# Pairing the 64-row ends of a 1728-wide feed-forward, with a longer backward lag

## The chip, the core and the metric

The kernel runs on one core of a Trainium2 chip. Its engines are TensorE (matmul, with a weight load ahead of each matmul), VectorE, ScalarE, GpSimd (POOL) and SyncE, which here only issues DMAs. TensorE writes to PSUM, an accumulator memory, from which VectorE and ScalarE read; everything else lies in SBUF, or in the chip's main memory. The metric is the device time of one execution in microseconds, as a median of several runs.

## The reference

A gated mix of two blocks, run forward and backward in one kernel. x and grad_out are 2048 x 640, all in bf16:

```python
g = sigmoid((x * gate_w).sum(-1, keepdims=True))
a = linear_attention(x, wqkv, wo)      # 32 heads of 20; phi(t) = t+1 or exp(t)
b = relu(x @ w1) @ w2                  # w1 640 x 1728, w2 1728 x 640
out = g * a + (1 - g) * b
```

The outputs are `out` and the gradients of the sum against grad_out: for x, wqkv, wo, w1, w2 and gate_w (`out_0` to `out_6`, in that order).

## The kernel before

The 2048 tokens are 16 tiles of 128 (NT), 640 is 5 blocks of 128 (KD), and F = 1728 is 13 blocks of 128 and one of 64 (KF = 14, FT = 64). The hidden activations of a tile, `hs(i)`, are kept padded to 14 x 128 = 1792 columns; the pad is set to zero by a memset for each group of four tiles (L501). w2's 14th block is padded by a memset (L385), and so is w1's transposed tail (L452, L636).

`mm_cols` (L315) is one product of a stationary 128x128 block with 640 columns: two matmuls, of 512 and 128 columns, into the two banks of one accumulator. Accumulators come from one pool of four, `pp()` (L288). Large SBUF buffers are placed in one arena by a planner from sizes and lifetimes that are written by hand (L116 to L183), in rings of 2 to 4 slots where they rotate.

Stages, in order:
- K chunks and the product Y (L412 to L454), with w1's tail transposed by TensorE in between (L448 to L453).
- Forward, L546 to L558: for each tile `q_main`, `h_half(i, 0)`, `q_post`, `h_half(i, 1)`, then `out_chunk(i - 2)` (LAG = 2). `h_half` ends with a transposing DMA of `hs(i)` into `hTs[i]` (L514), and `out_chunk` multiplies the 14 blocks of it by w2, and five of `pqTs[i]` by M, into one accumulator. `q_store` writes three pairs of tiles through SyncE.
- dW2, L608 to L627: for each of 14 blocks m, 16 tiles are accumulated (L611); between blocks run `r_main` and `r_post`, the start of the attention backward. `r_main` copies a 128x32 result on VectorE (L582).
- X, L637 to L648: five blocks, each sent to `load_T(XT_s...)` at once. Then three more transposing loads, KV2, woT, wvT (L649 to L651).
- Feed-forward backward, L756 to L778: for each tile `fb_a(i)` (two halves of `gp`, masked on VectorE in place of `hs(i)`, then a transposing DMA to `dhTs[i]`), and `fb_b(i - 2)`, 14 blocks of it by w1T into `dp`. Four groups of small products, `small_0` to `small_3`, with the DMAs that they lead to, stand at i = 2, 3, 5 and 8. In the last two rounds `dw1_half` takes `fb_a`'s place.
- dW1 and `dk_chunk` (L779 to L790), dWk, dWq, and dx (L825 to L849), where the last tile's two column parts share one accumulator.

SyncE's transposes and loads go through one queue, ScalarE's stores through another, each in order. The order on a queue is not always that of the text: the tile framework plans each engine's order ahead of time, and moves DMAs forward where it can.

The loop that the diff reorders most, as it stands before:

```python
for i in range(NT + LAG):
    if i < NT:
        fb_a(i)
    else:
        dw1_half(i - NT)
    ...
    if i >= LAG:
        fb_b(i - LAG)
```

Of the kernel before, what the change touches and what calls it, by code (L numbers as in the profile page):

```python
# [77 lines left out]
def kernel(  # L78
# [73 lines left out]
    ar.add("X", KD * D * B2, T_X, T_FB + 22)  # L152
    ar.add("XT", KD * D * B2, T_X + 5, T_FB + 25)
    ar.add("KV2", KD * D * B2, T_FB, T_FB + 22)
    ar.add("woT", KD * D * B2, T_FB, T_FB + 25)
    ar.add("wvT", KD * D * B2, T_FB + 5, T_FB + 45)
    ar.add("YT", KD * D * B2, T_FB + 30, T_FB + 60)
    ar.add("dKV", KD * D * B2, T_FB + 30, T_FB + 60)
    ar.add("dKVT", KD * D * B2, T_FB + 22, T_FB + 45)
    ar.add("Q", KD * D * B2, T_FB + 25, T_DWK - 10)  # L160
    ar.add("N", KD * D * B2, T_DWK, T_END)
    ring("hTb", KF * P, 3, T_FB, T_DW1 + 5)
    ring("wst", D, 4, T_FB, T_FB + 60)
    ar.add("dwoT", KD * D * B2, T_FB + 10, T_FB + 50)
    ar.add("dwo", KD * D * B2, T_FB + 22, T_FB + 60)
# [219 lines left out]
    nc.gpsimd.memset(w2_s[:, KF - 1, :], 0.0)  # L385
    nc.sync.dma_start(w2_s[:FT, KF - 1, :], B_w2[(KF - 1) * P:F, :])

# [47 lines left out]
    for m in range(KD):  # L435
# [12 lines left out]
        if m == 2:  # L448
            tp = psp.tile([P, KD, P], BF16, tag="PP", bufs=4, name="w1ttp")
            for k in range(KD):  # L450
                nc.tensor.transpose(tp[:FT, k, :], w1_s[:, k, (KF - 1) * P:F], ident[:])
            nc.vector.memset(w1T_tail[:], 0.0)  # L452
            nc.vector.tensor_copy(w1T_tail[:FT, :], tp[:FT].rearrange("p k d -> p (k d)"))  # L453
# [45 lines left out]
    def h_half(i, half):  # L499
        if i % G == 0 and half == 0:  # L500
            nc.gpsimd.memset(hsg[i // G][:, :, F:FPAD], 0.0)  # L501
# [9 lines left out]
        else:  # L511
            nc.vector.tensor_scalar(dst, hp[:, :, 0:NBW], omg_t[:, i:i + 1], 0.0, ALU.mult, ALU.max)
            hTs[i] = rnext("hTf").rearrange("p (c s) -> p c s", s=P)
            load_T(hTs[i], hs(i))  # L514

    def out_chunk(i):
        pr, ii = i // 2, i % 2
        op = pp("op")
        hT, pqT = hTs.pop(i), pqTs.pop(i)
        for kf in range(KF):  # L520
            mm_cols(op, hT[:, kf, :], lambda a, e: w2_s[:, kf, a:e], kf == 0, False)
        for k in range(KD):
            mm_cols(op, pqT[:, k, :], lambda a, e: M_s[:, k, a:e], False, k == KD - 1)
# [22 lines left out]
    for i in range(1, NT + LAG):  # L546
        if i < NT:
            q_main(i)
            h_half(i, 0)
            q_post(i)  # L550
            h_half(i, 1)
        if i % 2 == 0 and i <= NT:
            q_store(i // 2 - 1)
        if i >= LAG:
            out_chunk(i - LAG)
        if i == NT - 1:
# [12 lines left out]
    def r_main(i):  # L569
# [12 lines left out]
        nc.vector.tensor_copy(doX[:, i, D:DX], w32[:])  # L582
# [25 lines left out]
    for m in range(KF):  # L608
        wp = pp("w2p")
        for i in range(NT):  # L610
            mm_cols(wp, hs(i)[:, csl(m)], lambda a, e: doX[:, i, a:e], i == 0, i == NT - 1)  # L611
        st = rnext("w2st")
        nc.scalar.copy(st, flat(wp)[:, 0:D])
        rows = P if m < KF - 1 else FT
        nc.scalar.dma_start(out_5[m * P:m * P + rows, :], st[:rows, :])
        while 0 < m and done < NT and done < m * NT / (KF - 3):
# [20 lines left out]
    for m in range(KD):  # L637
# [10 lines left out]
        load_T(XT_s[:, :, csl(m)], X_s[:, m, :])  # L648
    load_T(KV2_s, KVT_d)  # L649
    load_T(woT_s, A_wo)  # L650
    load_T(wvT_s, A_wqkv[:, 2 * D:3 * D])  # L651
# [4 lines left out]
    def fb_a(i):  # L656
        for half in range(2):
            gp = pp("gp")
            for nb in range(2):
                blk = 2 * half + nb  # L660
                for k in range(KD):
                    nc.tensor.matmul(gp[:, nb, 0:NBW], lhsT=doTg[i // G][:, k, gsl(i)],  # L662
                                     rhs=w2T_s[:, k, blk * NBW:(blk + 1) * NBW], start=(k == 0), stop=(k == KD - 1))
            rng = slice(2 * half * NBW, (2 * half + 2) * NBW)
            gs = tmp("tb", 8, [P, 2, NBW])
# [219 lines left out]
```

## Time and profile before

| what | value |
|---|---|
| median of 3 runs | 658.83 us (658.72 to 659.83) |
| the profiled execution | 659.8 us, of which the span of the trace is 657.9 |
| granted TensorE clock over the span | 0.995 |
| DMA | 108.19 MB moved; SyncE's queue took 59.5% of the 16 engines' span |

Busy time of each engine by stage (us from the start; TensorE is PE):

| stage | stretch | PE | VectorE | ScalarE | POOL | DMA share |
|---|---|---|---|---|---|---|
| K chunks | 0 to 34 | 31.6 of 34.0 | 24.8 | 15.0 | 26.0 | 0.98 |
| Y | 34 to 61 | 23.0 of 27.0 | 19.9 | 2.3 | 5.4 | 0.57 |
| forward | 69.5 to 227.1 | 157.6 of 157.6 | 70.8 | 36.4 | 61.3 | 0.65 |
| X | 311.2 to 334 | 22.8 of 22.8 | 1.8 | 3.5 | 0.0 | 0.44 |
| dW1, dk | 477 to 545 | 68.0 of 68.0 | 24.3 | 6.7 | 0.0 | 0.59 |
| dWk, dWq | 545 to 588.7 | 43.7 of 43.7 | 3.1 | 7.1 | 0.0 | 1.09 to 1.13 |
| dx | 588.7 to 657.9 | 65.7 of 69.2 | 25.0 | 1.0 | 0.0 | 0.13 |

Between these lie dW2 (227.1 to 311.2; PE 82.8 of 84.1, VectorE 55.2, ScalarE 20.6) and the feed-forward backward (334 to 477; PE 140.1 of 143.0, VectorE 35.6, ScalarE 52.0, DMA share 0.83).

How to read it: matmuls are pipelined, and one lasts longer in the records (379 ns for 512 columns, 219 for 128) than it keeps the next one waiting. So the pace of TensorE is read from the distance of starts. A line such as `170.92 5.33 PE L317 MATMUL op_1823<-arena ... x38` is a group of 38 matmuls that started at 170.92 us, over 5.33 us. In brackets behind such a line stand the idle time before it and what ended it. "arena" names any buffer of the large SBUF block. A wait is put down to whichever of its releasers came last.

### The profile page before, as it was taken

The page shows a single profiled execution, that of the slowest core. Times are in us where ns is not written, and L with a number is a line of the kernel's source. Part 1 is how long each engine was busy: PE and PEld are TensorE (multiplying, and loading weights), DVE is VectorE, ACT ScalarE, POOL GpSimd, SP SyncE. Part 2 cuts the span into 40 slices and gives each one's busy share as a digit, 9 for nine tenths or more (in the row PEclk, how much of TensorE's full clock was granted, in tenths as well). Part 3 has the DMA queues.
Part 4 walks back from the last instruction along what each step waited for, and adds up shares of the span by engine and source line. Part 5 has one row for each costly group of instructions (what it writes and reads, how often), then busy time and mean ns, then how long its engine had stood idle before and what let it go on. Part 6 is the DMA issues. An engine that isn't in the chain of part 4 may idle for free.

```text
span 657.9 us, 10575 instructions
## 1 busy us (share of the span) xinstructions
PE 643.6 (98%) x4475; PEld 362.2 (55%) x4475; DVE 266.3 (40%) x503; ACT 148.1 (23%) x193; POOL 120.3 (18%) x115
## 2 busy tenths in 40 slices
PE   8979999999999999999999999999999999999997
PEld 5546555555555555555555545555555555555554
DVE  5994654445445137785034322222043320104442
ACT  4401321222212122322133435333101111020000
POOL 6931444334343112332001000000000000000000
PEclk9979999999999999999999999999999999999999
DMA  9991863664738999326389999934186439991111
GB/s 258 319 354 60 212 159 101 146 153 122 177 74 227 280 239 253 115 81 155 81 171 192 271 256 277 237 81 96 53 190 121 118 92 225 215 254 41 41 41 41
DMA packets 229049, 108.19 MB, mean 164 GB/s; under 512 B 181770, under 2 KB 228362, under 8 KB 229002
## 3 DMA queue, kind: packets, MB, share of 16 engines
q1 hardware_dynamic: 217114, 92.93, 59.5%
q10 hardware_dynamic: 11888, 14.59, 7.0%
q8 instruction: 35, 0.57, 0.4%
q14 instruction: 12, 0.10, 0.0%
HBM read 31.46 MB, written 30.97 MB: 95 GB/s over the span
## 4 chain that ended last, share of the span: by engine, by line
PE 87%; DMA 5%; DVE 5%; issue 1%; SPq 1%; ACT 1%; ACTq 0%; DVEq 0%
DMA arena<-arena 3%; DVE arena L362 2%; PE yp_531 L317 1%; PE w1p_5247 L750 1%; PE w1p_5122 L750 1%; PE w1p_4985 L750 1%; PE w1p_5190 L750 1%; PE w1p_5054 L750 1%; PE w1p_4916 L750 1%; PE w1p_4847 L750 1%; PE w1p_4761 L750 1%; PE w1p_4661 L750 1%; PE w1p_4596 L750 1%; DMA arena<-pqg_d 1%; PE op_2304 L317 1%
## 5 line engine op out<-in xcount | busy, mean ns | idle before, releaser
L317 PEld LDWEIGHTS <-arena 128*128 128x128 bf16 x2914 | 226.3, 98 | 183.4 <-issue 9.0
L750 PEld LDWEIGHTS <-arena 128*128 128x128 bf16 x320 | 30.9, 98 | 26.6
L662 PEld LDWEIGHTS <-arena 128*128 128x128 bf16 x320 | 30.7, 98 | 26.4
L506 PEld LDWEIGHTS <-arena 128*128 128x128 bf16 x320 | 30.6, 98 | 26.2
L406 POOL TENSOR_TENSOR arena<-arena 128x640 f32<-128x640 f32 x14 | 19.7, 1409 | 5.1 <-DVE arena L362 4.4
L641 PEld LDWEIGHTS <-arena 128*128 128x128 bf16 x80 | 7.8, 98 | 9.4
L815 PEld LDWEIGHTS <-arena 128*128 128x128 bf16 x80 | 7.8, 98 | 9.5
L828 DVE SCALAR_TENSOR_TENSOR f_5652<-gwb,dl_t,arena 128x640 f32<-128x640 bf16 x1 | 0.9, 884 | 28.7 <-DMA arena<-dxB_d 28.7
L693 POOL MEMSET arena<- 128x3200 bf16 x1 | 2.8, 2764 | 40.0 <-PE dwo_3583 L339 40.0
L734 DVE TENSOR_TENSOR tb_4739<-dkp_4728,dzb 128x640 bf16<-128x640 f32 x1 | 0.8, 825 | 22.8 <-PE dkp_4728 L317 22.8
L317 PE MATMUL yp_489<-arena 128*128 128x512 bf16 (+1 forms) x32 | 4.9, 308 | 4.0 <-DVE arena L362 4.0
L339 PEld LDWEIGHTS <-arena 128*128 128x128 bf16 x140 | 7.8, 97 | 1.9 <-issue 0.8
L642 PEld LDWEIGHTS <-arena 128*128 128x128 bf16 x80 | 7.8, 98 | 0.0
L816 PEld LDWEIGHTS <-arena 128*128 128x128 bf16 x80 | 7.8, 98 | 0.0
L317 PE MATMUL yp_531<-arena 128*128 128x512 bf16 (+1 forms) x32 | 6.6, 387 | 0.0
L750 PE MATMUL w1p_4596<-arena 128*128 128x432 bf16 x32 | 6.0, 346 | 0.0
L750 PE MATMUL w1p_4916<-arena 128*128 128x432 bf16 x32 | 6.0, 346 | 0.0
L750 PE MATMUL w1p_4985<-arena 128*128 128x432 bf16 x32 | 6.0, 346 | 0.0
L750 PE MATMUL w1p_5122<-arena 128*128 128x432 bf16 x32 | 6.0, 346 | 0.0
L750 PE MATMUL w1p_5247<-arena 128*128 128x432 bf16 x32 | 6.0, 346 | 0.0
L750 PE MATMUL w1p_4661<-arena 128*128 128x432 bf16 x32 | 6.0, 346 | 0.0
L750 PE MATMUL w1p_4761<-arena 128*128 128x432 bf16 x32 | 6.0, 346 | 0.0
(1026 smaller groups left out, 1208.4 us busy)
## 6 DMA issues: line engine op xcount, KB each, us to landing
out_dram<-arena ACTq DMA_DIRECT2D x28, 160.0 KB, 3.9
pk_d<-arena SPq DMA_DIRECT2D x4, 640.0 KB, 9.6
arena<-in_grad_out_dram SPq DMA_DIRECT2D x8, 320.0 KB, 4.6
pqg_d<-arena SPq DMA_DIRECT2D x8, 320.0 KB, 4.4
e_d<-arena SPq DMA_DIRECT2D x8, 320.0 KB, 4.0
out_dram<-arena ACTq DMA_DIRECT2D x8, 320.0 KB, 3.4
arena<-pqg_d SPq DMA_DIRECT2D x4, 640.0 KB, 5.5
arena<-e_d SPq DMA_DIRECT2D x8, 320.0 KB, 3.5
```

The costliest lines, as they stand in the source:

```text
L317: nc.tensor.matmul(ps_tile[:, b, 0:e - a], lhsT=lhsT, rhs=rhs_fn(a, e), start=start, stop=stop, **kw)
L339: nc.tensor.matmul(ps_tile[:, bank, a - 512 * bank:e - 512 * bank], lhsT=lhsT_fn(j), rhs=rhs_mat[:, j, a:e], start=bank not in seen, stop= ...
L362: nc.vector.scalar_tensor_tensor(dst, ps_flat, 1.0 + 1e-6, cp[:], ALU.add, ALU.max)
L406: nc.gpsimd.tensor_tensor(zacc, zacc, pkN[:, i, :], ALU.add)
L506: nc.tensor.matmul(hp[:, nb, 0:NBW], lhsT=xT(i, k), rhs=w1_s[:, k, blk * NBW:(blk + 1) * NBW], start=(k == 0), stop=(k == KD - 1))
L641: nc.tensor.matmul(xp[:, 0, :], lhsT=lhsT, rhs=doX[:, i, 0:512], start=(i == 0), stop=(i == NT - 1))
L642: nc.tensor.matmul(xp[:, 1, 0:DX - 512], lhsT=lhsT, rhs=doX[:, i, 512:DX], start=(i == 0), stop=(i == NT - 1))
L662: nc.tensor.matmul(gp[:, nb, 0:NBW], lhsT=doTg[i // G][:, k, gsl(i)], rhs=w2T_s[:, k, blk * NBW:(blk + 1) * NBW], start=(k == 0), stop=(k ...
L693: nc.gpsimd.memset(dKVT_s, 0.0)
L750: nc.tensor.matmul(wp[:, nb, 0:NBW], lhsT=xN2[:, i, csl(m)], rhs=hs(i)[:, blk * NBW:(blk + 1) * NBW], start=(i == 0), stop=(i == NT - 1))
L815: nc.tensor.matmul(wp[:, 0, :], lhsT=lhsT, rhs=dqN[:, i, 0:512], start=(i == 0), stop=(i == NT - 1))
L816: nc.tensor.matmul(wp[:, 1, 0:D + 1 - 512], lhsT=lhsT, rhs=dqN[:, i, 512:D + 1], start=(i == 0), stop=(i == NT - 1))
```

## The change

The pad of `hs(i)` and of w2's and w1T's last block is no longer zero but a second copy of the 64 real rows. The 14th block of two neighbouring tiles is then multiplied in one go: `tail_pair` uses partitions 0 to 63 for the even tile and 64 to 127 for the odd one, into two accumulators. In dW2's last block even tiles write accumulator rows 0 to 63 and odd tiles rows 64 to 127, and the halves are added afterwards. In the forward loop, `h_half(i, 1)` of odd tiles moves behind `out_chunk`. In the backward loop the lag becomes four tiles, with a ring of five for dhT, `fb_a` is called by halves, and the transposes and stores around the small products are spread over the iterations. `r_main` starts one block later, its 128x32 copy goes to ScalarE, and the last tile's second part gets its own accumulator. Lifetimes in the arena follow (most of those lines are left out here).

```diff
-    ar.add("X", KD * D * B2, T_X, T_FB + 22)
-    ar.add("XT", KD * D * B2, T_X + 5, T_FB + 25)
+    ar.add("X", KD * D * B2, T_X, T_FB + 24)
+    ar.add("XT", KD * D * B2, T_FB + 5, T_FB + 50)
...
-    ring("hTb", KF * P, 3, T_FB, T_DW1 + 5)
-    ring("wst", D, 4, T_FB, T_FB + 60)
-    ar.add("dwoT", KD * D * B2, T_FB + 10, T_FB + 50)
-    ar.add("dwo", KD * D * B2, T_FB + 22, T_FB + 60)
+    ring("hTb", KF * P, 5, T_FB, T_DW1 + 5)
+    ring("wst", D, 4, T_FB + 88, T_FB + 112)
...
-    nc.gpsimd.memset(w2_s[:, KF - 1, :], 0.0)
     nc.sync.dma_start(w2_s[:FT, KF - 1, :], B_w2[(KF - 1) * P:F, :])
+    nc.sync.dma_start(w2_s[FT:, KF - 1, :], B_w2[(KF - 1) * P:F, :])
...
                 nc.tensor.transpose(tp[:FT, k, :], w1_s[:, k, (KF - 1) * P:F], ident[:])
-            nc.vector.memset(w1T_tail[:], 0.0)
-            nc.vector.tensor_copy(w1T_tail[:FT, :], tp[:FT].rearrange("p k d -> p (k d)"))
+                nc.tensor.transpose(tp[FT:, k, :], w1_s[:, k, (KF - 1) * P:F], ident[:])
+            nc.vector.tensor_copy(w1T_tail[:], tp.rearrange("p k d -> p (k d)"))
...
     def h_half(i, half):
-        if i % G == 0 and half == 0:
-            nc.gpsimd.memset(hsg[i // G][:, :, F:FPAD], 0.0)
...
+            nc.vector.tensor_copy(hs(i)[:, F:FPAD], hs(i)[:, F - FT:F])
             hTs[i] = rnext("hTf").rearrange("p (c s) -> p c s", s=P)
             load_T(hTs[i], hs(i))
...
+    def tail_pair(psA, psB, lA, lB, rhs, last):
+        for b, (a, e) in enumerate(DSPL):
+            nc.tensor.matmul(psA[:, b, 0:e - a], lhsT=lA[0:FT], rhs=rhs[0:FT, a:e], start=False, stop=last)
+            nc.tensor.matmul(psB[:, b, 0:e - a], lhsT=lB[FT:P], rhs=rhs[FT:P, a:e], start=True, stop=False)
+    ops = {}
     def out_chunk(i):
         pr, ii = i // 2, i % 2
-        op = pp("op")
         hT, pqT = hTs.pop(i), pqTs.pop(i)
-        for kf in range(KF):
-            mm_cols(op, hT[:, kf, :], lambda a, e: w2_s[:, kf, a:e], kf == 0, False)
+        if ii == 0:
+            ops[i] = pp("op")
+        op = ops.pop(i)
+        for kf in range(KF - 1):
+            mm_cols(op, hT[:, kf, :], lambda a, e: w2_s[:, kf, a:e], ii == 0 and kf == 0, False)
         for k in range(KD):
-            mm_cols(op, pqT[:, k, :], lambda a, e: M_s[:, k, a:e], False, k == KD - 1)
+            mm_cols(op, pqT[:, k, :], lambda a, e: M_s[:, k, a:e], False, ii == 1 and k == KD - 1)
+        if ii == 0:
+            ops[i + 1] = pp("op")
+            tail_pair(op, ops[i + 1], hT[:, KF - 1, :], hTs[i + 1][:, KF - 1, :], w2_s[:, KF - 1, :], True)
         if ii == 0:
             o_st[pr] = rnext("ost").rearrange("p (i d) -> p i d", i=2)
         nc.scalar.copy(o_st[pr][:, ii, :], flat(op)[:, 0:D])
@@ -548,11 +560,14 @@
             q_main(i)
             h_half(i, 0)
...
-            h_half(i, 1)
+            if i % 2 == 0 or i == NT - 1:
+                h_half(i, 1)
         if i % 2 == 0 and i <= NT:
             q_store(i // 2 - 1)
         if i >= LAG:
             out_chunk(i - LAG)
+        if i < NT - 1 and i % 2 == 1:
+            h_half(i, 1)
...
-        nc.vector.tensor_copy(doX[:, i, D:DX], w32[:])
+        nc.scalar.copy(doX[:, i, D:DX], w32[:])
...
+        if m < KF - 1:
+            for i in range(NT):
+                mm_cols(wp, hs(i)[:, csl(m)], lambda a, e: doX[:, i, a:e], i == 0, i == NT - 1)
+            nc.scalar.copy(st, flat(wp)[:, 0:D])
+            nc.scalar.dma_start(out_5[m * P:(m + 1) * P, :], st)
+        else:
+            for i in range(0, NT, 2):
+                for b, (a, e) in enumerate(DSPL):
+                    for t in range(2):
+                        nc.tensor.matmul(wp[t * FT:(t + 1) * FT, b, 0:e - a], lhsT=hs(i + t)[:, m * P:F],
+                                         rhs=doX[:, i + t, a:e], start=(i == 0), stop=(i == NT - 2),
+                                         skip_group_check=True)
+            w2e = tmp("f32", 3, dt=FP32)
+            w2o = tmp("f32", 3, dt=FP32)
+            nc.scalar.copy(w2e[:], flat(wp)[:, 0:D])
+            nc.scalar.dma_start(w2o[0:FT, :], w2e[FT:P, :])
+            nc.gpsimd.tensor_tensor(st[0:FT, :], w2e[0:FT, :], w2o[0:FT, :], ALU.add)
+            nc.scalar.dma_start(out_5[m * P:F, :], st[0:FT, :])
+        while 1 < m and done < NT and done < (m - 1) * NT / (KF - 4):
...
-        load_T(XT_s[:, :, csl(m)], X_s[:, m, :])
     load_T(KV2_s, KVT_d)
-    load_T(woT_s, A_wo)
-    load_T(wvT_s, A_wqkv[:, 2 * D:3 * D])
...
+    def fb_a(i, half):
...
+        if half == 1:
+            nc.vector.tensor_copy(hs(i)[:, F:FPAD], hs(i)[:, F - FT:F])
+            dhTs[i] = rnext("hTb").rearrange("p (c s) -> p c s", s=P)
+            load_T(dhTs[i], hs(i))
     def fb_b(i):
         pr, ii = i // 2, i % 2
-        dp = pp("dp")
         dT = dhTs.pop(i)
-        for kf in range(KF):
-            mm_cols(dp, dT[:, kf, :], lambda a, e: w1T_s[:, kf, a:e], kf == 0, kf == KF - 1)
         if ii == 0:
+            ops[i] = pp("dp")
+        dp = ops.pop(i)
+        for kf in range(KF - 1):
+            mm_cols(dp, dT[:, kf, :], lambda a, e: w1T_s[:, kf, a:e], ii == 0 and kf == 0, ii == 1 and kf == KF - 2)
+        if ii == 0:
+            ops[i + 1] = pp("dp")
+            tail_pair(dp, ops[i + 1], dT[:, KF - 1, :], dhTs[i + 1][:, KF - 1, :], w1T_s[:, KF - 1, :], True)
             dx_st[pr] = rnext("dxst").rearrange("p (i d) -> p i d", i=2)
...
-        nc.sync.dma_start(dwoT_d.rearrange("(k p) d -> p k d", p=P), dwoT_s)
...
-        nc.sync.dma_start(dKVT_d.rearrange("(k p) d -> p k d", p=P), dKVT_s)
-        load_T(dwo_s, dwoT_d)
...
-        load_T(dKV_s, dKVT_d)
-        load_T(YT_s, Y_d)
-        nc.sync.dma_start(out_3.rearrange("(i p) d -> p i d", p=P), dwo_s)
-        nc.sync.dma_start(Q_d.rearrange("(k p) d -> p k d", p=P), Q_s)
...
-    for i in range(NT + LAG):
+    LAGB = 4
+    for i in range(NT + LAGB):
         if i < NT:
-            fb_a(i)
+            fb_a(i, 0)
+            if i == 1:
+                for m in range(KD):
+                    load_T(XT_s[:, :, csl(m)], X_s[:, m, :])
+            if i == 2:
+                load_T(woT_s, A_wo)
+            if i == 5:
+                load_T(wvT_s, A_wqkv[:, 2 * D:3 * D])
+            if i == 3:
+                nc.sync.dma_start(dwoT_d.rearrange("(k p) d -> p k d", p=P), dwoT_s)
+            if i == 6:
+                nc.sync.dma_start(dKVT_d.rearrange("(k p) d -> p k d", p=P), dKVT_s)
+                load_T(dwo_s, dwoT_d)
+            if i == 8:
+                nc.sync.dma_start(Q_d.rearrange("(k p) d -> p k d", p=P), Q_s)
+                nc.sync.dma_start(out_3.rearrange("(i p) d -> p i d", p=P), dwo_s)
+                load_T(YT_s, Y_d)
+            if i == 10:
+                load_T(dKV_s, dKVT_d)
+            if i % 2 == 0 or i == NT - 1:
+                fb_a(i, 1)
         else:
             dw1_half(i - NT)
+        if i >= LAGB:
+            fb_b(i - LAGB)
+        if i < NT - 1 and i % 2 == 1:
+            fb_a(i, 1)
         if i == 2:
             small_0()
-        if i == 3:
+        if i == 5:
             small_1()
-        if i == 5:
+        if i == 7:
             small_2()
-        if i == 8:
+        if i == 12:
             small_3()
-        if i >= LAG:
-            fb_b(i - LAG)
...
-    for n in range(2, 2 * KD):
+    for n in range(LAGB, 2 * KD):
...
             for b, (a, e) in enumerate(DSPL):
+                dp = dp if b == 0 else pp("dxp")
                 for n, (lhsT, rhs) in enumerate(terms):
```

## The prediction

> **What bounds the kernel.** I read the page from the top, then TensorE's waits, then the timeline of the stages that the diff touches.
>
> ```profile
> span 657.9 us, 10575 instructions
> ...
> PE 643.6 (98%) x4475; PEld 362.2 (55%) x4475; DVE 266.3 (40%) x503; ACT 148.1 (23%) x193; POOL 120.3 (18%) x115
> ...
> PEclk9979999999999999999999999999999999999999
> ```
>
> TensorE is busy 643.6 of 657.9 us at its full granted clock but for the third slice, and the chain of waits gives it 87%. Two things can shorten such a kernel: fewer columns streamed through the array, or fewer of the 14.3 us in which it stands. TensorE's waits name most of those:
>
> ```profile
> PE yp_489 L317 <- DVE arena L362: 4.0, 1, 4.0
> PE dp_3997 L317 <- DMA arena<-arena: 1.4, 1, 1.4
> PE w2p_2678 L317 <- DVE tb_2614 L589: 1.3, 1, 1.3
> ...
> PE dp_3593 L317 <- DMA arena<-arena: 0.9, 1, 0.9
> PE dxp_6176 L842 <- DVE arena L844: 0.8, 1, 0.8
> ...
> PE dp_4301 L317 <- DMA arena<-arena: 0.3, 1, 0.3
> ```
>
> The columns are: who waits, for whom, us in total, times, longest. The first (4.0, before the Y product) lies where the diff changes nothing. The other five, 4.7 us together, all lie where it does.
>
> **The unit of saving.** In the forward feed-forward stage TensorE has no gaps, so starts give the true pace:
>
> ```profile
> 170.92 5.33 PE L317 MATMUL op_1823<-arena 128*128 128x512 bf16 x38
> 176.08 1.52 PE L317 MATMUL qp_1866<-arena 128*128 128x512 bf16 x10
> ```
>
> 176.08 - 170.92 = 5.16 us for 19 products of 640 columns (a 512 and a 128 each), 0.272 us per product. By the same reading a half of h or of gp takes 1.82 us, q_main 1.36, fb_b 3.80.
>
> **Part 1, the 64-row ends paired.** Today the 14th block of F is half zeros and costs each of 16 tiles a full 0.272 us, in out_chunk and again in fb_b. Afterwards two tiles share one such pass: rows 0 to 63 of the array for the one, 64 to 127 for the other. If both halves run at once, a pair saves 0.272 us; there are 8 pairs in each stage. But this uses the array in another shape than the products around it. The Trainium skill, "TensorEngine Tiling (Array Packing)", section "Key Properties", says that changing the tiling mode drains the TensorE. It gives no size. The trace has two such changes, both from 128 stationary columns to few and back:
>
> ```profile
> 49.82 1.85 PE L317 MATMUL yp_577<-arena 128*128 128x128 bf16 x13
> 51.60 0.47 PE L451 MATMUL w1ttp<-ident,arena 128*64 128x128 bf16 x5
> 52.00 2.29 PE L317 MATMUL yp_627<-arena 128*128 128x512 bf16 x15
> ...
> 592.76 0.22 PE L852 MATMUL gtp<-ident,gcol 128*5 128x128 bf16 x1
> 592.91 0.93 PE L317 MATMUL dxp_5692<-arena 128*128 128x512 bf16 x5
> ```
>
> gtp streams 128 columns, and the next product starts 0.15 us after it. A product of 128 columns otherwise holds the next back by 0.055 us (the five of w1ttp start over 51.60 to 51.85, where the group's end 52.07 less one matmul's 0.22 is the last start). So leaving the mode costs 0.095 us. Entering costs the same: yp_577's last starts at 49.82 + 1.85 - 0.22 = 51.45, w1ttp 0.15 later. In and out are 0.19 us per pair, against 0.272 to be won: 0.08 us is left if both halves start together. That is the rule against this change, and it eats two thirds of this part.
>
> Whether they start together no row shows. Lower end: the two halves follow each other, and a pair loses 0.19. Upper end: +0.08. The nearest row is the pair of w1ttp's first two weight loads after the drain, 0.03 us apart by their starts; with such an offset of the second half, 0.05 remains. The skill, "TensorE: Matmul & The Clock Gate", section "Measured speedup vs the span model", measured 3.07 times for four row tiles, 77% of ideal; 77% of two is 1.54, a pair would take 0.543/1.54 = 0.353 us, and 0.543 - 0.353 - 0.19 leaves nothing. Between 0.05 and 0, I take 0.04: 16 x 0.04 = **0.6 us saved** (bounds -3.0 and +1.3).
>
> **Part 2, the last block of dW2.** Here the pairing is by columns and all 16 tiles are in one run, so the mode changes once. The block takes 16 x 0.272 = 4.35 us; half of it plus 0.19 saves 1.98, and 1.54-fold speed saves 4.35 - 2.82 - 0.19 = 1.34. I take **1.7 us**. The sum of the two halves adds an ACT copy to f32, an ACT-issued DMA across partitions, a POOL add and the store. The store waits in ACT's queue for the add: some 0.7 (L613) + 3.9 (a store's landing) + 1.4 (POOL's L406) = 6 us, an estimate, and behind it is the first X copy (L643), wanted 4.6 us later. It comes perhaps 1.5 us late, and with four accumulators TensorE doesn't meet it: nothing.
>
> **Part 3, lag four and the transposes spread out.** fb_b waits for dhT three times (0.9 + 1.4 + 0.3 = 2.6 us). What delays them is the queue in front:
>
> ```profile
> 376.12 7.82 SPq L307 DMA_TRANSPOSE arena<-in_A_x_dram  x2
> ...
> 384.67 3.87 SPq L307 DMA_TRANSPOSE arena<-arena  x1
> ...
> 390.95 3.98 PE L317 MATMUL dp_3997<-arena 128*128 128x512 bf16 x28 [1.36 <-DMA arena<-arena]
> ```
>
> Two xS transposes hold SP's queue for 7.82 us, dhT is issued at 384.67, takes 6.2 us to land by the chain of waits, and dp_3997 starts 1.36 late. Today from the end of fb_a(i) to fb_b(i) there are 3.80 + 3.65 + 3.80 + 3.65 = 14.9 us. Afterwards an even tile has 29.8 before fb_b needs it; its odd partner, wanted at the tail, has 7.45 + 7.45 + 3.65 + 3.53 = 22.1. At least 7 us more, over five times the longest lateness. Nothing is taken off SP's queue: XT's five, woT, wvT, dwo, YT, dKV and the stores of dwoT, dKVT and Q are issued all the same, later, each at least one iteration of 7.45 us before the product that reads it (XT i = 1 and woT 2 for small_1 at 5; wvT 5 for 7; YT 8 and dKV 10 for 12). **2.6 us saved.** The stage's DMA engines are 83% busy, so I cannot exclude a new wait (below).
>
> **Part 4, the dr chain.** One L582 cast of 128x32 takes 1.24 to 1.25 us in ten of 16 cases and 0.18 in five; the long ones stand beside POOL:
>
> ```profile
> 255.50 1.38 POOL L581 TENSOR_TENSOR f_2586<-zb,grd_2584 128x640 f32<-128x640 bf16 x1 [4.68 <-DVE grd_2584 L579]
> 255.67 1.25 DVE L582 CAST arena<-grd_2584 128x32 bf16<-128x32 f32 x1
> ```
>
> VectorE is held until POOL's tensor_tensor ends, and so r_post's L589, which frees the accumulator, comes 1.3 us late once. On ScalarE (20.6 us busy of the stage's 84) such a copy costs about 0.26 (gst, L853); there it waits for VectorE's w32 and holds back the next rb copy by some 0.6 us, which the four accumulators cover. **1.3 us saved.**
>
> **Part 5, the last tile.** With an accumulator of its own the second half needn't wait for L844's read: **0.8 us**, all of it at the end of the span.
>
> **What is added.** Five more transposes of w1's tail: 0.28 us if in turn, nothing if side by side; I take 0.15. A copy of 128x64 into the pad for each tile and stage, 32 on VectorE: between 0.1 and 1.25 us each (L582's two cases), hidden, as VectorE is 45% busy in the forward stage and 25% in the backward one. Seven dk_chunks in a row after dw1_half(4): TensorE 7 x 1.36 = 9.5 us, VectorE about 7 x 1.65 = 11.6; the accumulators absorb most. The second accumulator of a pair is held for half an iteration; three are left for q and h, each emptied within 1.7 us while TensorE works 1.8 on the next. The memsets removed were hidden, the added 80 KB load of w2's end is wanted 60 us later. For all this together, 0 to 2 us: I take 0.5.
>
> Sum: 0.6 + 1.7 + 2.6 + 1.3 + 0.8 - 0.15 - 0.5 = 6.3 us. The profiled execution took 659.8 us (its span 657.9 and 1.9 around it) and would take 653.5; the median of the runs is 1.0 lower, 658.83, so **652.5 us**. Likeliest case's own range: 650.5 to 654.5.
>
> **Rivals.** (a) The backward stage only exchanges its waits: SP's order is the framework's planner's (the trace has dq's load, written at L789, issued at 383.99), and with 83% DMA a moved transpose comes late for its small product instead. For: KVT's, Y's and xS's transposes take 6 to 8 us to land. Against: 15 us of distance. 2.6 back: 655.1. Chance 0.17.
> (b) The halves don't run at once. Then 16 pairs lose 3.0 instead of gaining 0.6, dW2 loses 0.2 instead of gaining 1.7: 652.5 + 3.6 + 1.9 = 658.0. Against: separate rows and separate accumulator banks. Chance 0.08.
> (c) Slower: the odd tile's hT in the forward stage. Its h_half now ends the iteration, and the even tile's tail waits for it 1.36 + 1.82 + 1.82 + 18 x 0.272 = 9.9 us later. The chain is L512's 1.02, the pad copy, and issue to landing, median 3.9 in this stage: 5.1 us, not late. But with the copy at 1.25, q_store's three issues ahead of it (2.6 us at 115.9 to 118.7) and a landing of 6.4 (the longest of dhT in the chain) it is 11.3, 1.4 late in each of 8 pairs: 652.5 + 11.3 = 663.8. It decides from 9.9 us on, and passes the old time when each pair is late by 0.8. Chance 0.12.
> (d) More is won, as the small products' own waits for accumulators (some 1.4 us by their starts) and the full 0.08 per pair fall in too: 649.8. Chance 0.08. The forecast has 0.55.
>
> A change of 0.2% (1.3 us) is about what a measurement can tell here. Faster: forecast, (a), (d) and a part of (b), 0.82; same, the rest of (b), 0.06; slower, (c), 0.12. From 649.0 to 658.5 the range holds all but (c) and a little.
>
> **What would show it.** In the timeline, psA and psB starting within 0.03 us, and about 0.15 from the product before to the pair and from the pair to the next; w2p's last group near 2.4 us instead of 4.35; no dp, w2p or dxp in TensorE's waits. A wait of op on a transpose would make (c) right; dwo, bd, qqp or dwv waiting for DMA, (a); a pair of 0.54 us, (b). The forecast is wrong if the forward stage's iteration exceeds 10.17 us.

## The result and the profile after

The kernel after took **655.44 us** (median of four runs, 653.99 to 655.69), the kernel before on the same chip 659.33 (658.72 to 661.03): a ratio of 0.9932, 95% interval 0.9908 to 0.9957. The prediction was 652.5 us against 658.83. So the direction was right, and of 6.3 us some 4 came: the time lies in the wide range (649.0 to 658.5) and above the likeliest case's own (650.5 to 654.5). The profiled execution took 655.64 us, its span is 4.0 us shorter. Its page, the counts and the clock first:

```profile
span 653.9 us, 10503 instructions
...
PE 636.0 (97%) x4400; PEld 357.6 (55%) x4480; DVE 262.6 (40%) x518; ACT 150.8 (23%) x209; POOL 120.7 (18%) x111
...
PEclk9979999999999999999999999999999999999999
```

TensorE's waits in the kernel after (who waits, for whom, us in total, times, longest):

```profile
PE yp_489 L317 <- DVE arena L362: 4.0, 1, 4.0
PE rp_2479 L317 <- DMA arena<-in_grad_out_dram: 3.3, 1, 3.3
PE warm_113 L376 <- DVE arena L366: 1.3, 1, 1.3
PE w2p_2814 L317 <- DVE tb_2750 L604: 1.2, 1, 1.2
```

The waits of dp and dxp are gone, as foretold. A wait of w2p is still there, at another block, and rp_2479 is new: the first dr product of dW2's stage stands for the transposed dO. Cut at the starts of the stages' first products, the two spans differ like this:

| stage | before, us | after, us | difference |
|---|---|---|---|
| start to the second q | 69.37 | 69.49 | +0.12 |
| forward | 157.71 | 157.23 | -0.48 |
| dW2 | 84.12 | 85.49 | **+1.37** |
| X | 22.80 | 22.81 | 0.0 |
| feed-forward backward, with two dw1 halves | 142.60 | 138.54 | **-4.06** |
| dw1 and dk to dWq | 111.99 | 111.99 | 0.0 |
| dx | 69.32 | 68.33 | -0.99 |

In the kernel after the backward loop holds two more halves of dw1; they are counted at 11.68 us in the row where they were before (150.22 - 11.68 = 138.54, and 100.31 + 11.68 = 111.99). The stages but for the start and dW2 repeat within some 0.1 us from run to run, and the kernel before's backward stage within 0.34 (142.94 in cast_alone, which doesn't change it), so that a single profile tells a few tenths there. dW2's stage varies more: left as it is in the kernel after, it took 85.46, 85.61 and 86.34 us in three later runs (rows_unpaired, lag_two, pair_in_turn), in each of them longer than before.

**The pairs.** One pair of the forward stage in the timeline (start, us, engine, line, output):

```profile
83.79 0.76 PE L317 MATMUL op_956<-arena 128*128 128x128 bf16 x5
84.49 0.39 PE L518 MATMUL op_956<-arena 64*128 64x512 bf16 x1
84.49 0.39 PE L519 MATMUL op_993<-arena 64*128 64x512 bf16 x1
84.71 0.22 PE L518 MATMUL op_956<-arena 64*128 64x128 bf16 x1
84.72 0.22 PE L519 MATMUL op_993<-arena 64*128 64x128 bf16 x1
84.86 1.48 PE L317 MATMUL qp_1001<-arena 128*128 128x512 bf16 x9
```

In all 16 pairs the odd tile's half starts 3 or 4 ns after the even tile's, and the pair begins 0.152 us after the last matmul before it. The next product starts 0.378 us after the pair. With 0.097 us for the entry (0.152 less the usual 0.055) a pair costs 0.475 us where two products cost 0.543: 0.068 us won by starts, 0.06 by the stage (0.48 / 8).

**dW2's last block.** The tile view of the kernel after shows the block's 32 matmuls, each on half the columns:

```profile
L635 PE MATMUL w2p_3229<-arena x32: 219/299/403, 309.9 to 312.1; 128*64 128x512 bf16 x16, 128*64 128x128 bf16 x16
```

From its start to the next product it takes 2.30 us, where the full block takes 4.35; the entry costs another 0.09, so 1.96 us are won. The stage lost 1.37 all the same, so 3.3 went elsewhere in it.

**The new wait.** SyncE's queue at the end of the forward stage, before:

```profile
221.49 0.77 SPq L310 DMA_DIRECT2D arena<-e_d  x1
222.31 0.76 SPq L310 DMA_DIRECT2D arena<-pqg_d  x1
228.39 7.71 SPq L307 DMA_TRANSPOSE arena<-in_grad_out_dram  x2
236.19 0.53 SPq L310 DMA_DIRECT2D arena<-e_d  x1
```

and after:

```profile
222.43 0.96 SPq L310 DMA_DIRECT2D arena<-pqg_d  x1
223.65 3.75 SPq L310 DMA_DIRECT2D arena<-e_d  x3
230.38 0.36 SPq L310 DMA_DIRECT2D arena<-pqg_d  x1
230.83 15.64 SPq L307 DMA_TRANSPOSE arena<-in_grad_out_dram  x3
```

Before, the first transposed group of dO was issued at 228.39, behind one load of e and one of pqg, and landed at 234.76. After, two more loads of e and a second load of pqg stand ahead of it. That pqg load was issued at 230.38, 0.07 us after the store of e at L495 had landed (230.31). dO follows at 230.83 and lands at 243.16, 12.3 us after its issue instead of 6.4. The product that reads it moved one block later with the diff (ready at 239.9 instead of 235.8), but its data 8.4 us later:

```profile
235.41 4.51 PE L317 MATMUL w2p_2444<-arena 128*128 128x512 bf16 x31
243.20 1.53 PE L317 MATMUL rp_2479<-arena 128*128 128x512 bf16 x10 [3.28 <-DMA arena<-in_grad_out_dram]
```

No line of the diff in dW2's stage touches these loads. What moves them is the arena. Worked out from the lifetimes in the two kernels by the kernel's own placement code, dO's first group and the ring of e lay before on buffers of the forward stage's post-processing (pqst, pqT); after, they lie on M and on w2, which the last `out_chunk` reads, and pqg lies on the stores' buffers of e. The diff changes lifetimes of the backward stage alone, but the plan is made anew for all. Two programs that were built and not run separate the plan from the rest of the diff: the kernel before with the new lifetimes alone has SyncE's DMAs at this place in the order of the kernel after, and the kernel after with `r_main` in its old place keeps that order.

### The profile page after: what moved, and what is told of

Its sections match the earlier page's. It is cut to its first block, busy times and chain, and to the rows that moved or that the text cites. A ratio compares the mean times of both kernels' runs of the same rounds, so it can differ in the third digit from the quotient of the medians.

```text
span 653.9 us, 10503 instructions
## 1 busy us (share of the span) xinstructions
PE 636.0 (97%) x4400; PEld 357.6 (55%) x4480; DVE 262.6 (40%) x518; ACT 150.8 (23%) x209; POOL 120.7 (18%) x111
## 4 chain that ended last, share of the span: by engine, by line
PE 87%; DVE 4%; SPq 3%; DMA 3%; issue 1%; ACT 1%; POOL 0%; DVEq 0%; ACTq 0%; POOLq 0%
SPq L307 3%; DMA arena<-in_grad_out_dram 2%; DVE arena L362 2%; PE yp_531 L317 1%; PE w1p_4639 L773 1%; PE w1p_4770 L773 1%; PE w1p_5090 L773 1%; PE w1p_4867 L773 1%; PE w1p_4571 L773 1%; PE w1p_5283 L773 1%; PE w1p_5226 L773 1%; PE w1p_5158 L773 1%; PE w1p_5021 L773 1%; PE w1p_4702 L773 1%; PE op_2315 L317 1%
## 5 line engine op out<-in xcount | busy, mean ns | idle before, releaser
L317 PEld LDWEIGHTS <-arena 128*128 128x128 bf16 x2818 | 219.0, 98 | 179.6 <-issue 11.0
L773 PEld LDWEIGHTS <-arena 128*128 128x128 bf16 x320 | 30.8, 98 | 26.9 <-issue 0.5
L686 PEld LDWEIGHTS <-arena 128*128 128x128 bf16 x320 | 30.5, 98 | 26.7 <-issue 1.3
L504 PEld LDWEIGHTS <-arena 128*128 128x128 bf16 x320 | 30.4, 98 | 25.8
L669 PEld LDWEIGHTS <-arena 128*128 128x128 bf16 x80 | 7.8, 98 | 9.6 <-issue 0.3
L861 PEld LDWEIGHTS <-arena 128*128 128x128 bf16 x80 | 7.8, 98 | 9.5
L339 PEld LDWEIGHTS <-arena 128*128 128x128 bf16 x140 | 7.9, 97 | 2.1 <-issue 1.0
L317 PE MATMUL yp_489<-arena 128*128 128x512 bf16 (+1 forms) x32 | 4.9, 308 | 4.0 <-DVE arena L362 4.0
L862 PEld LDWEIGHTS <-arena 128*128 128x128 bf16 x80 | 7.8, 98 | 0.0
L670 PEld LDWEIGHTS <-arena 128*128 128x128 bf16 x80 | 7.8, 98 | 0.0
L317 PE MATMUL yp_531<-arena 128*128 128x128 bf16 (+1 forms) x31 | 6.6, 387 | 0.1
L773 PE MATMUL w1p_4639<-arena 128*128 128x432 bf16 x32 | 6.0, 346 | 0.0
L773 PE MATMUL w1p_4770<-arena 128*128 128x432 bf16 x32 | 6.0, 346 | 0.0
L773 PE MATMUL w1p_4571<-arena 128*128 128x432 bf16 x32 | 6.0, 346 | 0.0
L773 PE MATMUL w1p_4867<-arena 128*128 128x432 bf16 x32 | 6.0, 346 | 0.0
L773 PE MATMUL w1p_5090<-arena 128*128 128x432 bf16 x32 | 6.0, 346 | 0.0
L773 PE MATMUL w1p_5226<-arena 128*128 128x432 bf16 x32 | 6.0, 346 | 0.0
```

What stands on the lines that cost most here:

```text
L317: nc.tensor.matmul(ps_tile[:, b, 0:e - a], lhsT=lhsT, rhs=rhs_fn(a, e), start=start, stop=stop, **kw)
L339: nc.tensor.matmul(ps_tile[:, bank, a - 512 * bank:e - 512 * bank], lhsT=lhsT_fn(j), rhs=rhs_mat[:, j, a:e], start=bank not in seen, stop= ...
L504: nc.tensor.matmul(hp[:, nb, 0:NBW], lhsT=xT(i, k), rhs=w1_s[:, k, blk * NBW:(blk + 1) * NBW], start=(k == 0), stop=(k == KD - 1))
L669: nc.tensor.matmul(xp[:, 0, :], lhsT=lhsT, rhs=doX[:, i, 0:512], start=(i == 0), stop=(i == NT - 1))
L670: nc.tensor.matmul(xp[:, 1, 0:DX - 512], lhsT=lhsT, rhs=doX[:, i, 512:DX], start=(i == 0), stop=(i == NT - 1))
L773: nc.tensor.matmul(wp[:, nb, 0:NBW], lhsT=xN2[:, i, csl(m)], rhs=hs(i)[:, blk * NBW:(blk + 1) * NBW], start=(i == 0), stop=(i == NT - 1))
```

## Experiments

Theory at the start: the arena's new plan and the order on SyncE's queue delay dO, and the wait of w2p is VectorE's or a buffer's. Rivals: the copy that was moved to ScalarE; a wait that only moves on. Each kernel's spans are compared by stage, as the start varies by 2 us from run to run (59.7 to 61.9).

**dot0_first.** The first transposed group of dO is issued ahead of e and pqg; in the last tile's chunk the products with M come first, so that its buffer is free earlier.

```diff
...
+    load_T(doTg[0], do2[0:G * P, :])
     e_load(0)
...
-        load_T(doTg[g], do2[g * G * P:(g + 1) * G * P, :])
+        if g > 0:
+            load_T(doTg[g], do2[g * G * P:(g + 1) * G * P, :])
```

> The changed kernel with the five M products of the last out_chunk ahead of its w2 products, and the transpose doT0 ahead of the three e loads on SyncE's queue. Theory A (doT0 came late because it stood behind three e loads and a pqg load): doT0 is issued near 226 instead of 230.8 us and lands by 236, rp_2479's wait of 3.3 us falls below 0.5, the span falls from 653.9 to about 650.6. Theory B (the stage's DMA engines are the limit, whatever the order): another transfer comes late instead, a wait on e or pqg at VectorE reaches TensorE, and the span stays above 652.9.

656.36 us (ratio 0.9950, 0.9917 to 0.9983). The transposed load went out at 222.98, was being issued for 9.46 us and landed at 236.58; rp's wait fell from 3.3 us for a DMA to 0.2 us for VectorE. But the stage took 85.21 us, only 0.3 less than the kernel after. In the waits of this kernel stand:

```profile
PE w2p L317 <- DVE tb L609: 3.9, 2, 2.0
PE rp L317 <- DVE tb L609: 0.2, 1, 0.2
```

The wait had moved on. ScalarE's timeline shows where to:

```profile
239.05 0.69 ACT L636 CAST arena<-w2p 128x640 bf16<-128x640 f32 x1 [3.75 <-PE w2p L317]
242.29 0.34 ACTq L637 DMA_DIRECT2D out_dram<-arena  x1
242.72 1.29 ACT L594 CAST tb<-rp 128x640 bf16<-128x640 f32 x2 [2.98 <-DMA arena<-pqg_d]
```

The store of a finished dW2 block (L637) reads what L636 wrote by 239.74, yet it is issued at 242.29, and the copies of dr (L594) behind it stand 2.98 us "for the load of pqg", which they do not read. That load landed at 242.21. By the operands in the trace both DMAs carry the same completion semaphore (a counter that tells of a DMA's landing), one of eight that the DMAs of both queues share, 32 DMAs each. Ahead of the store stands, as an instruction of its own, a wait for that semaphore, which ended at 242.23: this program doesn't issue a DMA until the one that used its semaphore last has landed. On ScalarE's queue such a store holds up the copies behind it.

**dq_three** (a third buffer for dq's pairs, behind the arena; its diff is the one shown under both_sp) and **cast_back** (the 128x32 copy on VectorE again), each alone on the kernel after:

```diff
-        nc.scalar.copy(doX[:, i, D:DX], w32[:])
+        nc.vector.tensor_copy(doX[:, i, D:DX], w32[:])
```

> The changed kernel with a third slot for the dq staging ring, in arena space that was free; the order of instructions on every engine is the same. Theory C (w2p_2814 waits 1.2 us because VectorE's L607 waits 1.4 us for a dq store to land, and with it the L604 behind it): that wait goes, the span falls by 1.2 to about 652.7. Theory D (the wait comes from ScalarE, whose rb copy is 1.3 us late behind a store that waits for a w2T transpose's semaphore): it stays within 0.4 of 1.2.

> The changed kernel with the 128x32 copy (L597) back on VectorE. The prediction's step (the copy on VectorE causes the 1.3 us wait in dW2): the casts take 1.24 us beside POOL again, and w2p's wait grows from 1.2 to about 2.5, the span to 655.2. Rival (VectorE has slack there, the wait is set by DMA landings): waits in dW2 stay within 0.3 us, span 653.6 to 654.2.

658.18 and 657.43 us, one run each; dW2's stage 87.46 and 86.87 us. In neither is a wait of w2p listed, but neither is decisive: rp's wait was 4.1 and 3.4 us, and from within it on the granted clock stood at half for 6.8 us, which makes the stage longer and gives VectorE time. The windows of dq_three (us, busy of each engine; PEclk is the last but two):

```profile
236.00:242.50 6.50, 4.46 (x34) 2.36 (x31) 0.00 (x0) 1.39 (x2) 0.00 (x0) 1.00 1.27 171
242.50:249.50 7.00, 4.91 (x19) 2.43 (x20) 1.26 (x2) 0.69 (x1) 0.00 (x0) 0.53 1.21 211
```

**cast_alone.** The kernel before with only the copy of Part 4 moved to ScalarE, the diff of cast_back the other way round.

> The kernel before with this copy on ScalarE and nothing else. The prediction's step: w2p_2678's wait of 1.3 us goes, and the span falls from 657.9 to 656.6. Rival (ScalarE's rb copy, held 2 us by a store that waits for a w2T transpose, sets it, and the cast on ScalarE adds to its queue): the wait stays above 0.8 us, the span within 0.5 of 657.9.

659.25 us, one run. The wait of w2p fell from 1.3 to 0.5 us:

```profile
PE w2p L317 <- DVE tb L589: 0.5, 1, 0.5
```

The store of ScalarE still waited for a transposed load of w2: the copies behind it stood 2.49 us, and 2.63 in the kernel before, whose trace has this line:

```profile
252.12 0.69 ACT L574 CAST tb_2579<-rp_2568 128x640 bf16<-128x640 f32 x1 [2.63 <-DMA arena<-in_B_w_dram]
```

So by this one run the copy was part of the cause, worth some 0.8 us of the 1.3 (two profiles of one program differ by 0.6 in such a wait, see dot0_sp). The stage took 83.78 us, 0.34 less than before, as rp now waited 0.3 us.

**r_later.** The dr products begin one block later still.

```diff
-        while 1 < m and done < NT and done < (m - 1) * NT / (KF - 4):
+        while 2 < m and done < NT and done < (m - 2) * NT / (KF - 5):
```

> The dr products of dW2's stage begin one block of w2 rows later (4.35 us) and then come at a slightly faster rate; they end with the same block as in the kernel after. Theory (the stage lost 1.4 us because the first dr product stands 3.3 us for the first transposed group of dO, which lands at 243.2 in any case): the transposed group isn't moved, the product that reads it comes 4.4 us later than its old start of 239.9, so that TensorE's wait on it goes, the stage takes 85.5 - 3.3 = 82.2 us and the run 652.2 us. Rival (only the place of the wait is at issue: the faster rate makes VectorE and the copies late, and TensorE waits for a free accumulator): the wait on the DMA is gone as well, but waits of w2p on VectorE grow from 1.2 to 3 us or more, and the stage stays above 84.5.

657.28 us (ratio 0.9972, 0.9952 to 0.9991), the stage 87.90 us: worse, and the theory's 652.2 fell. The wait for dO is gone; in its place rp stands 4.3 us for an accumulator, and from near the end of that wait the clock is at half for 6.8 us. ScalarE's timeline:

```profile
245.45 0.69 ACT L629 CAST arena<-w2p 128x640 bf16<-128x640 f32 x1 [3.65 <-PE w2p L317]
252.90 0.34 ACTq L630 DMA_DIRECT2D out_dram<-arena  x1
253.33 1.29 ACT L589 CAST tb<-rp 128x640 bf16<-128x640 f32 x2 [7.20 <-DMA arena<-pqg_d]
```

The same picture as in dot0_first, for 6.8 us: the store drew the semaphore of a load of pqg that landed at 252.82. The rival had named VectorE's and the copies' rate; the trace shows the store.

**store_sp.** The kernel after, with that store on SyncE. TensorE, VectorE and POOL run the same instructions in the same order.

```diff
-            nc.scalar.dma_start(out_5[m * P:(m + 1) * P, :], st)
+            nc.sync.dma_start(out_5[m * P:(m + 1) * P, :], st)
```

> The kernel after, with the stores of dW2's blocks (L630) issued by SyncE in place of ScalarE; TensorE, VectorE and POOL run the same instructions in the same order. In the kernel after the store at 265.31 stood 1.4 us in ScalarE's queue until a transposed load of w2, the DMA that last used the same completion semaphore, had landed, and the copies of dr behind it stood with it. Theory (two causes in a row: the copies on ScalarE are late by this store, and after them L607 on VectorE waits until the store of dq, issued behind four transposes of w2, has landed at 269.7): the stall of ScalarE goes, but the wait for dq stays, so TensorE's wait of w2p on VectorE stays at 0.8 to 1.2 us; the wait of rp on the transposed dO (3.3 us) stays; the stage takes 85.2 to 85.5 us. Rival (the store alone made it late): no wait of w2p is left, and the stage takes 84.2.

653.29 us (0.9888, 0.9852 to 0.9924), the stage 83.54 us. The stall of ScalarE is gone; w2p's wait stays, for the cause that was expected:

```profile
PE w2p L317 <- DVE tb L604: 1.0, 1, 1.0
```

VectorE's timeline in this kernel:

```profile
268.58 0.49 DVE L607 TENSOR_TENSOR arena<-tb,arena 128x640 bf16<-128x640 bf16 x1 [2.24 <-DMA dq_d<-arena]
```

L607 writes the third pair of dq into a ring of two and waits for the first pair's store, which SyncE issues at 264.66, behind the transposes of w2. Not expected: rp's wait fell from 3.3 to 1.6 us. dO's first group now lands 10.0 us after its issue, not 12.3. In the kernel after two stores of dW2 blocks (232.18 and 236.34) ran beside it; here none does before 250.68. That these two made the difference fits, but no run tests it alone.

**dot0_sp.** Meant as dot0_first with the store on SyncE. Of dot0_first's edit it has the moved load alone, not the products with M ahead in the last tile's chunk.

> The kernel dot0_first (first transposed group of dO issued ahead of the loads of e and of pqg), with the stores of dW2's blocks issued by SyncE too. In dot0_first ScalarE's stores at 242.29 and 250.63 were issued 0.08 us after the landing of a load of pqg that had used the same completion semaphore, 2.5 and 2.2 us after the copy before them was done, and the copies of dr waited behind them; TensorE then waited 3.9 us for accumulators. Theory (these stalls in ScalarE's queue are what took the gain of dot0_first): the first of the two waits goes (2.0 us), the second, where the store of dq lands late, stays at 1 to 2 us; the stage goes from 85.2 to 83.2 us, the run to 654. Rival (the loads of pqg themselves are what the chain waits for, by whichever queue): the waits stay near 3.9 us and the stage at 85 us.

654.06 us (0.9896, 0.9860 to 0.9932), the stage 84.04 us, and not 83.2. Without that reordering dO's buffer comes free no earlier, the framework's planning put dO behind the loads of e and pqg again (issued at 231.84), and the program that results is the same as store_sp's, instruction for instruction. So neither the theory nor its rival is tested, and what an early dO is worth without the stalls stays open. What the run gives is a second profile of store_sp: dW2's stage took 83.54 us in one and 84.04 in the other, w2p's wait 1.0 and 1.6, rp's 1.6 and 1.5.

**both_sp.** dot0_sp, which is store_sp, with the third buffer of dq_three; each engine's order stays.

```diff
-    arena = arena_pool.tile([P, total // 2], BF16, name="arena")
+    arena = arena_pool.tile([P, total // 2 + 2 * D], BF16, name="arena")
...
-        o = ar.off(name) // 2 + (i % count) * elems
+        o = total // 2 if name == "dqst" and i % 3 == 2 else ar.off(name) // 2 + (i % (3 if name == "dqst" else count)) * elems
```

> dot0_sp with a third buffer for dq's pairs, so that VectorE's L607 no longer needs the store of dq that is issued behind the four transposes of w2. Theory (the three causes, dO's landing, the stores in ScalarE's queue, and dq's two buffers, are all there are): no wait of TensorE in the stage above 0.5 us, the stage takes 81 us (16 dr products of 1.36, 13 blocks of 4.35 and one of 2.3 make 80.5), the run 651.0 us, below both kernels. Rival (each wait that is removed is replaced by a wait on the next load in SyncE's queue, which now carries the stores too): the stage stays above 83 us.

**651.72 us** (0.9862, 0.9830 to 0.9894), below both kernels: its interval doesn't meet that of the kernel after, and its six runs (651.44 to 652.78) lie below all eight of store_sp and dot0_sp (653.23 to 654.80). The waits that are left:

```profile
PE yp L317 <- DVE arena L362: 4.0, 1, 4.0
PE rp L317 <- DMA arena<-in_grad_out_dram: 1.7, 1, 1.7
PE warm L376 <- DVE arena L366: 1.3, 1, 1.3
```

The stage takes 82.48 us, 1.06 less than store_sp and 1.56 less than dot0_sp, whose w2p waits were 1.0 and 1.6. With the stores off ScalarE's queue, then, the two buffers of dq were the whole of that wait. Without the 1.7 of rp it would reach 80.8, close to the 80.5 of its products alone (16 x 1.358 + 13 x 4.346 + 2.30). That last wait comes from where dO and e lie; an arena that puts them elsewhere was not tried, and the theory's 651.0 and "no wait above 0.5" were missed by it.

**lag_two.** The kernel after with a lag of two in the backward loop, transposes still spread.

```diff
-    LAGB = 4
+    LAGB = 2
```

> The kernel after with the backward feed-forward stage's lag of two tiles again, the small products' transposes at their new places. Theory (the longer distance is what the pairing needs, and the spreading alone would not have removed the waits): the odd tile's dhT is wanted 3.65 + 3.53 = 7.2 us after its gp, and its chain of activation, mask, product, pad copy and transpose takes 6 to 8 us; dp waits on DMA come back, in most of the 8 pairs, 3 to 10 us in all, and the stage from the first gp to the first dk goes from 150.2 (which holds two more half blocks of dw1, 11.7 us; here these stand behind dk) to 141.5 or more, where it would be 138.5 without waits. Rival (the transposes that stood ahead in SyncE's queue were the cause, and the lag was not): no dp wait above 0.3 us, 138.5.

661.65 us, one run, the backward stage 145.06 us against 138.54, and 142.60 in the kernel before. With a lag of two, pairing and spreading together lose time. The waits:

```profile
PE dp L519 <- DMA arena<-arena: 3.2, 3, 1.4
PE dp L317 <- DMA arena<-arena: 2.2, 1, 2.2
```

L519 is the odd half of a pair: its dhT comes late in three of eight pairs, where the distance is 7.2 us. The even half then runs alone:

```profile
368.24 0.39 PE L518 MATMUL dp<-arena 64*128 64x512 bf16 x1
369.66 0.39 PE L519 MATMUL dp<-arena 64*128 64x512 bf16 x1 [1.03 <-DMA arena<-arena]
369.66 0.23 PE L518 MATMUL dp<-arena 64*128 64x128 bf16 x1
```

The even half's 128 columns (369.66), issued behind the waiting product, wait with it. The 2.2 us of L317 are an even tile's, the first, whose dhT was issued behind the moved transposes of XT and woT. What spreading would do without the pairing, which alone brings the odd tile's 7.2 us, no run shows.

**rows_unpaired.** Full 128-row products for the last block of F again, the lower half of the weights zero.

```diff
...
-        for kf in range(KF - 1):
+        for kf in range(KF):
...
-            tail_pair(op, ops[i + 1], hT[:, KF - 1, :], hTs[i + 1][:, KF - 1, :], w2_s[:, KF - 1, :], True)
```

> The kernel after, with the last block of F again a full 128-row product for each of the 16 tiles (the lower half of the weights is zero), in the forward and in the backward feed-forward stage; everything else stays. Theory (a pair takes 0.48 us with its two changes of the array's shape, two full products 0.54): the forward stage goes from 157.23 back to 157.7, the backward one from 150.2 to 150.7, the span grows by 1.0 us. Rival (the prediction's 0.04 for a pair, or the 0 of the skill's page): 0.3 a stage, or nothing.

656.22 us, one run. The forward stage takes 157.71 us, as before the change: the eight pairs there are worth 0.48 us. The backward stage grows by 0.69; of this 0.48 are expected by the same count, and the rest goes with dwv, which is no longer issued between the products of dp.

**pair_in_turn.** The four products of a pair in the order even 512, even 128, odd 512, odd 128.

```diff
         for b, (a, e) in enumerate(DSPL):
             nc.tensor.matmul(psA[:, b, 0:e - a], lhsT=lA[0:FT], rhs=rhs[0:FT, a:e], start=False, stop=last)
+        for b, (a, e) in enumerate(DSPL):
             nc.tensor.matmul(psB[:, b, 0:e - a], lhsT=lB[FT:P], rhs=rhs[FT:P, a:e], start=True, stop=False)
```

> The kernel after, with the four products of a pair issued in the order even tile 512, even tile 128, odd tile 512, odd tile 128, in place of alternating tiles. Theory (the halves run at once only as far as the order of issue puts them side by side; a product behind one on the same rows waits, and all behind it): only the even tile's 128 columns still lie beside the odd tile's 512; a pair takes 0.21 us longer, 16 pairs 3.4 us, some 1.7 in each of the two stages. Rival (the array takes the odd tile's product past the waiting one): no change, 157.2 and 150.2.

655.94 us, one run; forward 157.26 us. The theory fell. The timeline of this kernel, where L520 is the odd tile:

```profile
83.66 0.39 PE L518 MATMUL op<-arena 64*128 64x512 bf16 x1
83.66 0.39 PE L520 MATMUL op<-arena 64*128 64x512 bf16 x1
83.88 0.21 PE L518 MATMUL op<-arena 64*128 64x128 bf16 x1
83.89 0.22 PE L520 MATMUL op<-arena 64*128 64x128 bf16 x1
```

The odd tile's 512 columns stand in the program behind the even tile's 128, and start 0.22 us before them, 5 to 8 ns after the even tile's 512 in all 16 pairs. A product that waits for its rows is passed by one for other rows; one that waits for a semaphore (lag_two) is not. The backward stage's 0.27 us more isn't in the pairs (0.381 to 0.382 each); dwv is again issued in other places.

## Why the prediction was right in sign and 3 us too low

- **Part 1, row pairs: right, undersized.** 0.6 foretold, 0.96 measured (2 x 0.48). The drains of 0.095 us at entry and exit, taken from w1ttp and gtp, hold to 2 ns. The mis-sized term is the offset of the second half: 0.03 taken, 0.004 measured. The 77% of ideal for four row tiles of the Trainium skill, "TensorE: Matmul & The Clock Gate", section "Measured speedup vs the span model", which would have made the gain nothing, is not what two 64-row tiles show here; that section's model, some 4 ns for each further tile, is.
- **Part 2, dW2's last block: right.** 1.7 foretold, 1.96 measured, the full-overlap value (1.98).
- **Part 3, lag and transposes: right, undersized.** 2.6 foretold; 3.6 came in the stage besides the pairs (4.06 - 0.48). dp's waits were 3.0 us by the distance of starts, where the waits' view has 2.6, and the small products' waits for accumulators went from 1.4 to 0.9. lag_two supports the reason given, distance: with the transposes spread and a lag of two, dp waits 5.4 us. How the gain divides between lag and spreading is not shown.
- **Part 4, the dr chain: wrong.** 1.3 foretold, 0.1 measured (a wait of 1.3 became one of 1.2). The step that failed is that VectorE, held until POOL's tensor_tensor ends, is the one reason why L589 comes 1.3 us late. cast_alone gives some 0.8 us for it, and the stall of ScalarE's copies (2.63 us) already stood in the kernel before's trace. In the kernel after two other links set the accumulator free: the store that holds ScalarE's queue, and the store of dq behind w2's transposes. Cure the first alone (store_sp) and 1.0 stays, 1.6 in the second profile; cure the second too (both_sp) and the wait is gone.
- **Part 5, the last tile: right.** 0.8 foretold, 0.99 measured, the whole of it at the end.
- **What is added: wrong in kind.** 0.65 was taken, for w1's transposes, the copies and the dk chunks. These cost 0.1 (a product of M's transposes waits 0.1 longer for VectorE); seven dk chunks in a row cost nothing, and w1ttp's ten transposes take the time of five. But 3.3 us came in at a place that the prediction doesn't mention: dO's load at the start of dW2. It read the diff's lifetimes for the stage they belong to, and looked for SyncE's new order there only; the loss in dW2 was put at nothing without a reason.

The measured parts make -0.96 - 1.96 - 3.6 - 0.1 - 0.99 + 3.3 + 0.1 = -4.2 us, against -4.0 in the span. That the time stayed in the range is in part luck: parts 1, 2, 3 and 5 gave 7.5 us where 5.7 were foretold, which made up for the 1.2 missing in part 4 and for some of the 3.3 that had no term in the sum. Of the rivals, none came as it was described: the time of (a), 655.1, was nearly met, but its mechanism fell with the dp waits, (b) with the starts 4 ns apart, (c) since no op waits for a transpose (an iteration of the forward stage takes 10.14 us, half of the 20.28 from one pair to the next). Of (d), the accumulators' part came about by a third and the pairs nearly in full, but both were outweighed by dW2.

## What to carry to other kernels

When buffers share one planned arena, a lifetime edited in one stage can delay loads in another: compare the plans of both kernels, and the order on each DMA queue at every stage boundary, before pricing a change at nothing elsewhere. Keep stores off the queue of an engine whose next instruction is on the chain; a DMA can stand there for a transfer that has nothing to do with it. A wait ended by an engine is often the last of several links: cure them together, or one run with a single cure will look as if its link had been innocent.

## What the runs showed that was not expected

- Products in separate halves of the rows start 3 to 8 ns apart even if another product, for busy rows, was issued between them (pair_in_turn). The same page of the skill, section "The mechanism", has matmuls start strictly in order; this measurement differs. Changing between full and half array costs 0.095 us each way.
- A wait of TensorE can cost more than its length, and where it falls decides. In all 13 traces every change of the granted clock up to the kernel's end lies on a grid of 3.41 us, whose phase differs from run to run (in dq_three 38.14, 44.97, 242.94 and 249.77). The clock falls to half at the end of a cell of that grid in which TensorE stood 2.0 us or more (17 falls, 2.0 to 3.4 us; one cell with 2.04, in the kernel after, brought none). It rises at the end of the first cell in which TensorE stood 0.7 us or less; cells with 0.9 to 2.0 us kept it at half. So the waits of 3.4, 3.9, 4.1 and 4.3 us in dW2's stage (cast_back, pair_in_turn, dq_three, r_later) brought half clock for 6.8, 3.4, 6.8 and 6.8 us. Those of 3.3 (after) and 3.8 (lag_two), which a border of the grid cuts into pieces of 2.04 us at most, brought none. The wait of 4.0 us for Y brings it in every trace, the kernel before's too. The Trainium skill, "TensorE: Matmul & The Clock Gate", section "What's actually happening", has a free-running window of some 3.4 us, with which the grid agrees, and half clock after an idle one; here the window need not be idle throughout.
- One transposing load, of the same data, can occupy SyncE for 7.4 or 9.5 us while it is issued (kernel after, dot0_first), and for 6.5 in store_sp, where it took 4.3 in the kernel before; everything behind it on the queue moves with it.
- In these programs an engine's DMA is held by the landing of an unrelated DMA of another queue that used the same completion semaphore: 2.5 us in dot0_first, 6.8 in r_later.
